# Unread products in TensorE's planned waits among the first pairs, and a plan in which GpSimd overlaps half of VectorE's two-operand passes

## Chip, cores and metric

The kernel runs on one core of a Trainium2 chip. The metric is the device time in microseconds (us) of that core, from an execution of the whole program. A profiled execution gives, beside its time, a trace of every instruction.

## What is computed

Attention with a sliding window of 128 keys and 4 sink keys, over 4 batches, 8 heads, 768 positions and head dimension 64; its result, laid side by side over the heads, goes through a two-layer network with squared ReLU. Cut to what matters:

```python
scores = q @ k.T / sqrt(64)
keep = (pos_k < n_sink) | ((0 <= pos_q - pos_k) & (pos_q - pos_k < window))
a = softmax(where(keep, scores, -1e9))
x = (a @ v), heads side by side          # 3072 x 512
h = maximum(x @ w_in, 0)                 # 512 x 2048
out = (h * h) @ w_out                    # 2048 x 512
```

The weights arrive as 64-bit numbers (w_in and w_out), the rest as 32-bit.

## The kernel before, in words

**Units of work.** The 3072 tokens are cut into 8 chunks of 384 tokens (half a batch), and each chunk has 4 pairs of heads, so there are 32 pairs. A pair's attention runs through: loads of q, k, v (lines 405, 410, 417); scores on TensorE (line 483 for the first eight pairs in plain fp32, line 489 for the others); a masked reduce on VectorE that also gives the row's minimum (line 466); the exponential on ScalarE (line 472); a sum and reciprocal on VectorE (lines 529, 530); the scaling of the rows on GpSimd or ScalarE (lines 537, 535); the sink columns on GpSimd (lines 552, 550); a transpose (by TensorE at lines 590 and 638 for the first two chunks, copied out of PSUM at line 600; later by VectorE and DMA); the product with the values (lines 726, 730); and the split of the result into a high and a low part, x (ScalarE line 742, VectorE line 747).

**The network.** Each chunk goes through 16 slices of the hidden dimension. A slice is a first product (12 matmuls, line 778), ReLU and square on ScalarE (lines 791, 795), two passes on VectorE (line 800, and line 807, which writes the low part gl), and a second product into three PSUM banks (9 matmuls, line 823; every third of them reads gl). After a chunk's last slice the three banks are copied out (line 864). The first chunk is run in two halves: slices 0 to 7, then all of the second chunk, then slices 8 to 15.

**The weights** are 32 rows of 64-bit words. VectorE turns each row into fp32 with three passes over integers (lines 303, 310, 317); ScalarE makes the rounded high part (line 323); and the low part is a subtraction (line 327) that the plan gives to VectorE or GpSimd, whichever it expects to be done first. All 32 rows are made while the first chunks are computed.

**Order.** Nothing is ordered by hand. The class Plan (from line 45) holds a list of steps, each with its engine and a cost in us written into the code, what it reads and writes, a rank, and the PSUM banks that it takes and gives back. Plan.order() plays the engines forward in time: it keeps the time when each engine is free, picks the step that can start first (by rank among those within 0.03 us), sets its start and end, and emits it. So each engine's instruction stream is written in the order in which the plan's own clock started the steps, and on the chip an engine runs its stream strictly in that order. Costs marked "port" are VectorE passes that use the SBUF port that VectorE shares with GpSimd. The plan lets such a pass and a GpSimd step exclude each other: whichever comes second starts when the first is over (lines 109, 110, 136 and 137):

```python
if e == "POOL" or "port" in kind:
    t = max(t, port["DVE" if e == "POOL" else "POOL"])
...
if e == "POOL" or "port" in kind:
    port[e] = t + cost
```

PSUM's eight banks are handed out by the plan too. Steps of the first chunk's pairs may take any of the eight; others take from three banks ("att"), the first products from two ("h") and the second from three ("o").

Of the kernel before, what the change touches and what calls it, by code (L numbers as in the profile page):

```python
# [18 lines left out]
P = 128  # L19
# [11 lines left out]
TOP_MAX = 2.0**16 * (2.0 - 2.0**-3 - 2.0**-23)  # L31
TOP_MIN = 2.0**-15 * 1.125
EPS = 1.0e-9
URGE = 0.5
LOW_DVE = 0.6
CP_DVE = 0.3
# [13 lines left out]
class Plan:  # L50
# [15 lines left out]
    def add(self, at, rank, emit, reads=(), writes=(), take=(), drop=()):  # L66
        n = len(self.steps)
        before = {self.writer[c] for c in (*reads, *writes) if c in self.writer}
        for c in writes:
            before.update(self.readers.get(c, ()))  # L70
        for c in reads:
            self.readers.setdefault(c, []).append(n)
        for c in writes:
            self.writer[c], self.readers[c] = n, []
        before.discard(n)
        for key in drop:
            self.left[key] = self.left.get(key, 0) + 1
        for b in before:
            self.steps[b]["after"].append(n)
        at = at if isinstance(at, list) else [at]  # L80
        self.steps.append(
            dict(at=at, rank=rank, emit=emit, take=take, drop=drop, after=[], waits=len(before), ready=0.0)
        )
# [12 lines left out]
    def order(self):  # L96
        free = dict(PE=0.0, DVE=5.5, ACT=1.5, POOL=5.0, SP=0.5)
        port, landed, mode, flow = {"DVE": 0.0, "POOL": 0.0}, [], 0, 0.0
        open_ = [n for n, s in enumerate(self.steps) if s["waits"] == 0]
        while open_:  # L100
            best = {}
            for n in open_:
                s = self.steps[n]
                ready, picks = self.able(s)
                if ready is None:
                    continue
                e, cost, *kind = min(s["at"], key=lambda o: max(ready, free[o[0]]) + o[1] + (o[3] if len(o) > 3 else 0.0))
                t = max(ready, free[e])
                if e == "SP" and len(landed) > 7:
                    t = max(t, landed[-8])  # L110
                if e == "POOL" or "port" in kind:
                    t = max(t, port["DVE" if e == "POOL" else "POOL"])
                best.setdefault(e, []).append((t, s["rank"], n, cost, kind, picks))
            chosen = None
            for e, able in best.items():
                first = min(able)[0]
                a = min((a for a in able if a[0] <= first + 0.03), key=lambda a: a[1:3])
                if chosen is None or a[0] < chosen[1][0]:
                    chosen = e, a
            e, (t, rank, n, cost, kind, picks) = chosen  # L120
            s = self.steps[n]
            open_.remove(n)
            for (pool, key), i in zip(s["take"], picks):
                self.got[key], self.since[i] = i, None
            if e == "PE":
                cost += 0.17 * (kind[0] != mode)
                mode = kind[0]
            free[e] = t + cost
            if e == "SP":
                flow = max(flow, t + 1.3) + kind[1] / RATE  # L130
                done = max(t + kind[0], flow + 0.7)
                landed.append(done)
                done += LATE
            else:
                done = t + cost + self.TAIL[e]
                if e == "POOL" or "port" in kind:
                    port[e] = t + cost
            for key in s["drop"]:
                self.left[key] -= 1
                if not self.left[key]:  # L140
                    self.since[self.got[key]] = done + self.HOP
            for a in s["after"]:
                x = self.steps[a]
                to_pe = x["at"][0][0] == "PE"
                x["ready"] = max(x["ready"], free[e] if to_pe and e == "PE" else done + (AHEAD if to_pe else self.HOP))
                x["waits"] -= 1
                if not x["waits"]:
                    open_.append(a)
            self.log.append((e, t, free[e], done, n, rank))
            yield (lambda: s["emit"](e)) if len(s["at"]) > 1 else s["emit"]  # L150
        assert all(not s["waits"] for s in self.steps)
# [3 lines left out]
def sink_window_attention_moe(  # L155
# [10 lines left out]
    nc = tc.nc  # L166
    B, NPAIR, _, S = q.shape
    H = 2 * NPAIR
    NROW, _, DM = w_rows.shape
# [11 lines left out]
    with ExitStack() as fast:  # L181
# [6 lines left out]
        def sb(tag, shape, dt=F32, name=None):  # L188

            name = name or tag  # L190
            if name not in made:
                made[name] = wp.tile(shape, dt, tag=tag, name=name)
            return made[name]

        banks = [ps.tile([P, 512], F32, name=f"bank{i}") for i in range(8)]
# [4 lines left out]
        ident = wp.tile([P, P], F32, name="ident")  # L200
# [6 lines left out]
        eps = wp.tile([P, 2 * NQ], F32, name="eps")  # L207
        nc.gpsimd.memset(eps, EPS)
        pari = sb("gl0", [P, 2, 2], I32, "pari")
# [59 lines left out]
        plan = Plan()  # L269
# [113 lines left out]
        def attention(s, rank):  # L383
# [79 lines left out]
            def reduce_(h, i, n, o, mask, key):  # L463
                ps_ = bank(key)
                nb = nbs[:, c * H + 2 * p + h, i : i + 1]
                nc.vector.tensor_tensor_reduce(  # L466
                    Pt(h)[:, i, o : o + n], ps_[:, 0:n], mask[:, 0:n], -SCALE, BIG, ALU.add, ALU.min, nb
                )

            def exp(h, i, n, o):  # L470
                nb = nbs[:, c * H + 2 * p + h, i : i + 1]
                nc.scalar.activation(  # L472
                    Pt(h)[:, i, o : o + n], Pt(h)[:, i, o : o + n], AF.Exp, bias=nb, scale=-1.0,
                    accum_out=sm[:, h, i : i + 1],
                )
# [25 lines left out]
            for m, (i, heads) in enumerate(order):  # L501
# [13 lines left out]
                for h, key in zip(heads, keys):  # L515
                    add(
                        ("DVE", 0.355 if n > P else 0.21), r - URGE,
                        lambda h=h, i=i, n=n, o=o, mask=mask, key=key: reduce_(h, i, n, o, mask, key),
# [4 lines left out]
                    add(  # L523
                        ("ACT", 0.5 if n > P else 0.4), r - URGE, lambda h=h, i=i, n=n, o=o: exp(h, i, n, o),
                        reads=[("nb", s, h, i), P_cell(h)], writes=[(P_cell(h), i), sm_cell, ("e", s, h, i)],
                    )

            def recip(hs):
                nc.vector.tensor_tensor(rs[:, hs], sm[:, hs], eps.rearrange("p (h i) -> p h i", h=2)[:, hs], op=ALU.add)  # L529
                nc.vector.reciprocal(rs[:, hs], rs[:, hs])  # L530

            def scale(engine, h, i, n, o):
                a = Pt(h)[:, i, o : o + n]
                if engine == "ACT":
                    nc.scalar.activation(a, a, AF.Copy, scale=rs[:, h, i : i + 1])
                else:
                    {"POOL": nc.gpsimd, "DVE": nc.vector}[engine].tensor_scalar(  # L537
                        a, a, rs[:, h, i : i + 1], 1.0, op0=ALU.mult, op1=ALU.mult
                    )
# [17 lines left out]
            for heads in groups:  # L557
                hs = slice(heads[0], heads[-1] + 1)
                r = rank(1.05 if plain or heads[0] else 1.45)
                add(  # L560
                    ("DVE", 0.22), r - URGE, lambda hs=hs: recip(hs),
                    reads=[("e", s, h, i) for h in heads for i in range(NQ)], writes=[(rs_cell, h) for h in heads],
                )
                for h in heads:
                    for i in range(NQ):
                        _, n, _, o = block(i)
                        pool = ("POOL", 0.46 if n > P else 0.33)
                        add(
                            [pool, ("ACT", 0.38 if n > P else 0.28, "", SC_ACT)] if plain else [pool, pool], r - URGE,
                            lambda e, h=h, i=i, n=n, o=o: scale(e, h, i, n, o),  # L570
# [3 lines left out]
                    add(  # L574
                        ("POOL", 0.29), r - URGE + 0.01, lambda h=h: part_sinks(h, False),
                        reads=done, writes=[(psk_cell, h)] + ([] if two == 0 else [psk_cell]),
                    )
                    add(
                        ("POOL", 0.32), r - URGE + 0.01, lambda h=h: part_sinks(h, True),
                        reads=done + [(psk_cell, h)], writes=[(psk_cell, h, 1)],  # L580
# [358 lines left out]
        def count():  # L939
# [10 lines left out]
            ("DVE", 0.1), END + 0.5, lambda: nc.vector.tensor_copy(flagi, bank("flag")[0:1, 0:1]), reads=["flag"],  # L950
            writes=["flagi"], drop=["flag"],
        )
        with tc.manual_schedule(engines={E.PE, E.DVE, E.Activation, E.Pool, E.SP}):
            for emit in plan.order():
                emit()
# [9 lines left out]
def general(  # L965
# [76 lines left out]
    with tc.For_i(0, B, 1) as b:  # L1042
        xT = one.tile([P, NPAIR, S], F32, name="gxT")
        for h in range(H):
# [9 lines left out]
            for i in range(NB):  # L1054
# [16 lines left out]
                nc.scalar.activation(sc, sc, AF.Exp, accum_out=st[:, 1:2])  # L1071
                nc.vector.tensor_scalar(st[:, 2:3], st[:, 1:2], EPS, None, op0=ALU.add)
                nc.vector.reciprocal(st[:, 3:4], st[:, 2:3])
# [86 lines left out]
```

## Time and profile before

| | |
|---|---|
| median of 3 runs | 691.01 us (689.49 to 691.43) |
| the profiled execution | 688.96 us |
| its span, first to last instruction | 686.9 us |
| TensorE matmuls busy | 667.4 us, 97% |
| VectorE busy | 459.1 us, 67% |
| ScalarE busy | 375.0 us, 55% |
| GpSimd busy | 215.2 us, 31% |
| mean granted TensorE clock | 0.991 |

In the profile PE is TensorE's matmuls, PEld its weight loads, DVE is VectorE, ACT ScalarE, POOL GpSimd, and SP the engine that issues the DMAs. A row of the timeline reads: start, duration, engine, line, operation, tiles written and read, how many instructions are merged, and in brackets the idle time before and what ended it. A row of the windows gives for a stretch of time the busy time of each engine with the number of instructions, then the granted TensorE clock (1.00 is full speed), the share of the DMA engines and GB/s. A product of two fp32 matrices is recorded as two matmuls (96 records at line 483 for 48 products in the program), a transpose as one (88 records at line 638 for 88 transposes).

### The profile page before, as it was taken

To read this page: it belongs to the slowest core of one execution; us is meant where nothing else is said; L and a number is where in the kernel's file an instruction comes from. 1 tells how busy PE (TensorE), PEld (TensorE's weight loads), DVE (VectorE), ACT (ScalarE), POOL (GpSimd) and SP (SyncE) were. 2 spreads that over 40 slices of the span, in tenths; PEclk is the share of its full clock that TensorE was granted. 3 is DMA by queue.
4 is the path that set the end of the run, shared out by engine and by line. 5 is a ranking of instruction groups with operands and counts; after the bars stand their busy time and mean duration, and the time that the engine had idled before them with its cause. 6 is when DMAs were issued, how large, how long until landed. Compare 5 with 4: busy or idle time off the path is not lost.

```text
span 686.9 us, 11380 instructions
## 1 busy us (share of the span) xinstructions
PE 667.4 (97%) x3722; PEld 581.1 (85%) x3722; DVE 459.1 (67%) x1194; ACT 375.0 (55%) x1073; POOL 215.2 (31%) x377
## 2 busy tenths in 40 slices
PE   4999989999999999999999999999999999999996
PEld 3667879998888888888888898888898888899985
DVE  7599999967987655676677766666776764242222
ACT  6798734355464434456666656666666565442221
POOL 4455433534544513232244323223332322000000
PEclk9799999999999999999999999999999999999999
DMA  7746455215777532466556666555557754310001
GB/s 244 220 163 203 168 192 183 84 52 157 223 245 227 154 106 93 134 207 193 155 148 184 211 188 201 170 167 174 145 169 213 223 160 114 116 51 12 0 1 51
DMA packets 58178, 104.78 MB, mean 153 GB/s; under 512 B 6208, under 2 KB 34624, under 8 KB 58112
## 3 DMA queue, kind: packets, MB, share of 16 engines
q1 hardware_dynamic: 58112, 103.98, 49.7%
q8 instruction: 31, 0.51, 0.3%
q14 instruction: 35, 0.29, 0.1%
HBM read 79.58 MB, written 24.38 MB: 151 GB/s over the span
## 4 chain that ended last, share of the span: by engine, by line
PE 90%; DVE 6%; ACT 1%; issue 1%; DMA 1%; SPq 0%; POOL 0%; DVEq 0%
PE bank L823 37%; PE bank L778 37%; PE bank L726 6%; PE bank L489 5%; PE bank L730 1%; DVE f L310 1%; PE bank L590 1%; PE bank L483 1%; DVE P L466 1%; PE bank L638 1%; DVE f L317 1%; DVE f L303 1%; DMA kn<-in_k_dram 1%; ACT w L323 0%; DVE w L327 0%
## 5 line engine op out<-in xcount | busy, mean ns | idle before, releaser
L778 PE MATMUL bank<-x,w 128*128 128x384 f32 x1536 | 303.1, 339 | 0.7 <-DVE gl L807 0.7
L778 PEld LDWEIGHTS bank<-x,w 128*128 128x128 f32 x1536 | 267.0, 188 | 9.5 <-issue 1.4
L823 PE MATMUL bank<-w,gh 128*128 128x512 f32 x768 | 242.7, 397 | 2.1 <-ACT ob L864 2.1
L823 PEld LDWEIGHTS bank<-w,gh 128*128 128x128 f32 x768 | 137.5, 188 | 21.4 <-ACT ob L864 2.4
L823 PE MATMUL bank<-w,gl 128*128 128x512 f32 x384 | 151.4, 394 | 0.0
L446 POOL TENSOR_TENSOR KS<-kn,KS 128x408 fp32r<-128x408 f32 (+1 forms) x48 | 64.9, 1352 | 225.1 <-DVE KS L441 164.2
L791 ACT ACTIVATE r<-bank 128x384 f32<-128x384 f32 x128 | 62.7, 490 | 129.3 <-PE bank L778 128.2
L472 ACT ACTIVATE P<-P,nbs 128x264 f32<-128x264 f32 (+1 forms) x192 | 94.4, 492 | 66.5 <-DVE nbs L466 65.7
L800 DVE TENSOR_TENSOR bank<-bank,r 128x384 f32<-128x384 f32 x128 | 72.1, 563 | 83.4 <-ACT r L791 83.1
L537 POOL TENSOR_SCALAR P<-P,small 128x128 f32<-128x128 f32 (+1 forms) x168 | 88.5, 543 | 71.1 <-DVE small L530 48.9
L823 PEld LDWEIGHTS bank<-w,gl 128*128 128x128 f32 x384 | 72.1, 188 | 16.6
L466 DVE CUSTOM_DVE_ANT_0 P<-bank,maskA 128x264 f32<-128x264 f32 x128 | 53.4, 426 | 45.1 <-PE bank L489 43.6
L807 DVE TENSOR_TENSOR gl<-bank,gh 128x384 fp32r<-128x384 f32 x128 | 70.9, 554 | 17.4 <-ACT gh L795 11.8
L795 ACT ACTIVATE gh<-r 128x384 fp32r<-128x384 f32 x128 | 66.7, 521 | 4.7 <-PE bank L823 2.2
L668 DVE STREAM_TRANSPOSE T<-P 128x384 f32<-128x384 f32 x96 | 45.2, 495 | 22.6 <-POOL P L537 21.7
L489 PEld LDWEIGHTS bank<-KS,QS 128*128 128x128 f32 x288 | 51.6, 188 | 6.2 <-DVE nbs L466 0.4
L489 PE MATMUL bank<-KS,QS 128*128 128x264 f32 (+1 forms) x288 | 55.4, 279 | 0.0
L742 ACT CAST x<-bank 128x384 fp32r<-128x384 f32 x32 | 15.3, 478 | 52.6 <-PE bank L730 52.4
L327 POOL TENSOR_TENSOR w<-f,w 128x512 fp32r<-128x512 f32 x19 | 27.1, 1430 | 51.4 <-ACT w L323 51.4
L726 PE MATMUL bank<-PT,vn 128*64 128x256 f32 (+1 forms) x392 | 40.6, 347 | 0.0
L726 PEld LDWEIGHTS bank<-PT,vn 128*64 128x64 f32 x392 | 25.7, 139 | 15.5 <-issue 6.7
L529 DVE TENSOR_TENSOR small<-small,eps 128x3 f32<-128x3 f32 (+1 forms) x56 | 34.5, 616 | 3.3 <-ACT P L472 2.7
(90 smaller groups left out, 575.5 us busy)
## 6 DMA issues: line engine op xcount, KB each, us to landing
raw<-in_moe_w_dram SPq DMA_DIRECT2D x32, 512.0 KB, 3.7
half<-in_moe_w_dram SPq DMA_DIRECT2D x64, 256.0 KB, 3.6
via<-T SPq DMA_DIRECT2D x48, 192.0 KB, 3.7
PT<-via SPq DMA_DIRECT2D x12, 768.0 KB, 4.4
via<-T SPq DMA_DIRECT2D x48, 160.0 KB, 4.2
PT<-via SPq DMA_DIRECT2D x12, 640.0 KB, 4.7
kn<-in_k_dram SPq DMA_DIRECT2D x24, 272.0 KB, 4.4
qn<-in_q_dram SPq DMA_DIRECT2D x32, 192.0 KB, 3.6
```

The source lines that it names most:

```text
L446: lambda h=h: nc.gpsimd.tensor_tensor(KS(h)[:, 1, 0:nk], kn()[:, h, 0:nk], f32(KS(h)[:, 0, 0:nk]), op=ALU.subtract),
L466: nc.vector.tensor_tensor_reduce(Pt(h)[:, i, o : o + n], ps_[:, 0:n], mask[:, 0:n], -SCALE, BIG, ALU.add, ALU.min, nb)
L472: nc.scalar.activation(Pt(h)[:, i, o : o + n], Pt(h)[:, i, o : o + n], AF.Exp, bias=nb, scale=-1.0, accum_out=sm[:, h, i : i + 1],)
L489: nc.tensor.matmul(bank(key)[:, 0:n], QS(h)[:, cols], flat[:, a, c0 : c0 + n], start=(a == 0), stop=(a == 1),)
L537: {"POOL": nc.gpsimd, "DVE": nc.vector}[engine].tensor_scalar(a, a, rs[:, h, i : i + 1], 1.0, op0=ALU.mult, op1=ALU.mult)
L726: nc.tensor.matmul(xo[h * D : h * D + D, qs[0] * P : qs[0] * P + len(qs) * P], vn[:, kk, h, :], rhs(), start=(n == 0), stop=False, skip_gr ...
L778: nc.tensor.matmul(bank(key)[:, 0:TOK], wi[fc][:, i, cc * P : (cc + 1) * P], xt[:, cc, :], start=(cc == 0 and j == 0), stop=(cc == NCC - 1 ...
L791: lambda key=key, r=r: nc.scalar.activation(r(), bank(key)[:, 0:TOK], AF.Relu),
L795: ("ACT", 0.41), n - 9, lambda gh=gh, r=r: nc.scalar.activation(gh(), r(), AF.Square),
L800: lambda key=key, r=r: nc.vector.tensor_tensor(bank(key)[:, 0:TOK], bank(key)[:, 0:TOK], r(), op=ALU.mult),
L807: lambda key=key, gh=gh, gl=gl: nc.vector.tensor_tensor(gl(), bank(key)[:, 0:TOK], f32(gh()), op=ALU.subtract),
L823: nc.tensor.matmul(bank(okey), gt()[:, ts_], wo[f][:, i, :], start=(f == f0 and j == 0), stop=(f == f1 - 1 and j == 2),)
```

## The change

There are two parts. Both sit in Plan.order().

1. When a TensorE step that takes a bank would start, by the plan's clock, before 24 us (WARM) and over 0.4 us after TensorE's step before it, the plan first emits fill(i, n): n fp32 products of the 128x128 identity with itself into the bank that the step is about to take. Nobody reads them; the step overwrites the bank. n is 70% of the planned wait (less 0.3 us) at 0.22 us a product. In the emitted program there are 33 such products: 20 ahead of the very first score, 1 ahead of the third pair's scores, and 12 among the first transposes. The plan's own clock isn't moved by them.
2. A GpSimd step, or a VectorE pass marked "port", holds the shared port for the plan only during the first half (SHARE) of its cost. No instruction is added, removed or resized by this, but every later choice of the plan can come out otherwise, so the streams of all engines are reordered from about the 20th instruction on, low passes go to other engines (line 327: VectorE 15 instead of 13, GpSimd 17 instead of 19), and 10 scalings go from ScalarE to GpSimd (line 537: 178 instead of 168; line 535: 14 instead of 24).

```diff
+WARM = 24.0
+SHARE = 0.5
...
             if e == "PE":
+                idle = t - free[e]
+                if picks and t < WARM and idle > 0.4:
+                    yield lambda i=picks[0], n=int((idle - 0.3) * 0.7 / 0.22): self.fill(i, n)
                 cost += 0.17 * (kind[0] != mode)
...
                 if e == "POOL" or "port" in kind:
-                    port[e] = t + cost
+                    port[e] = t + SHARE * cost
...
+        def fill(i, n):
+            for _ in range(n):
+                nc.tensor.matmul(banks[i][:, 0:P], ident, ident, start=True, stop=True)
+
+        plan.fill = fill
```

Three places in the streams show what moves. The lines of the changed kernel stand 5 further down up to the planner's callers and 10 at the end (line 960 is the new product). In names, the number behind the underscore at the end is a buffer's; P_1_0 and the like are a pair's probabilities, kn and qn its keys and queries, ident the identity.

TensorE, the start of its stream, before:

```order
L483 MATMUL bank0_67<-kn_0_146,qn_0_144 128x128
L483 MATMUL bank1_68<-kn_0_146,qn_0_144 128x128
L483 MATMUL bank2_69<-kn_0_146,qn_0_144 128x264
L483 MATMUL bank3_70<-kn_0_146,qn_0_144 128x264
L483 MATMUL bank4_71<-kn_0_146,qn_0_144 128x264
```

And now:

```order
L960 MATMUL bank0_67<-ident_78 128x128 x20
L488 MATMUL bank0_67<-kn_0_146,qn_0_144 128x128
L488 MATMUL bank1_68<-kn_0_146,qn_0_144 128x128
L488 MATMUL bank2_69<-kn_0_146,qn_0_144 128x264
L488 MATMUL bank3_70<-kn_0_146,qn_0_144 128x264
```

The first score stands behind 20 unread products.

ScalarE, where the third pair's exponentials (P_2) end, before:

```order
L472 ACTIVATE P_2_0_218,small_135<-P_2_0_218,nbs_125 128x264
L472 ACTIVATE P_1_198,small_135<-P_1_198,nbs_125 128x264
L472 ACTIVATE P_2_1_220,small_135<-P_2_1_220,nbs_125 128x264
L472 ACTIVATE P_2_0_218,small_135<-P_2_0_218,nbs_125 128x264
L472 ACTIVATE P_2_1_220,small_135<-P_2_1_220,nbs_125 128x264
L600 COPY PT_134<-bank2_69 128x512
```

And now (PT and SK are the copies of the first pair's transposes and of its sinks):

```order
L477 ACTIVATE P_2_0_239,small_135<-P_2_0_239,nbs_125 128x264
L477 ACTIVATE P_1_218,small_135<-P_1_218,nbs_125 128x264
L605 COPY PT_134<-bank2_69 128x512
L477 ACTIVATE P_2_1_241,small_135<-P_2_1_241,nbs_125 128x264
L605 COPY PT_134<-bank3_70 128x256
L605 COPY PT_134<-bank4_71 128x512
L540 ACTIVATE P_1_218<-P_1_218,small_135 128x264
L477 ACTIVATE P_2_0_239,small_135<-P_2_0_239,nbs_125 128x264
L605 CAST SK_0_132<-bank5_72 128x256
L477 ACTIVATE P_2_1_241,small_135<-P_2_1_241,nbs_125 128x264
```

The last three exponentials of the third pair stand behind the first pair's four copies.

VectorE, up to the fifteenth gl (line 807, now 812), which is slice 6 of the second chunk; f_28 is row 28 of the weights; before:

```order
L303 TENSOR_SCALAR f_28_1335<-raw_28_1260 128x512
L317 SCALAR_TENSOR_TENSOR f_27_1303<-raw_27_1219,f_27_1303 128x512
L310 SCALAR_TENSOR_TENSOR f_28_1335<-raw_28_1260,f_28_1335 128x512
L800 TENSOR_TENSOR bank4_71<-bank4_71,r_0_567 128x384
L807 TENSOR_TENSOR gl_0_590<-bank4_71,gh_0_578 128x384
```

And now:

```order
L322 SCALAR_TENSOR_TENSOR f_30_1352<-raw_30_1291,f_30_1352 128x512
L308 TENSOR_SCALAR f_31_1379<-raw_31_1312 128x512
L384 TENSOR_TENSOR VS_126<-vs_1_381,VS_126 16x512
L315 SCALAR_TENSOR_TENSOR f_31_1379<-raw_31_1312,f_31_1379 128x512
L805 TENSOR_TENSOR bank3_70<-bank3_70,r_0_630 128x384
L322 SCALAR_TENSOR_TENSOR f_31_1379<-raw_31_1312,f_31_1379 128x512
L812 TENSOR_TENSOR gl_0_653<-bank3_70,gh_0_635 128x384
```

The same product's low part stood behind weight rows up to 28 and now stands behind all 32, 0 to 31.

## The prediction

> **What bounds the kernel now.** I read TensorE's waits first, since its matmuls are busy 97% of the span. Columns: who waits for what, total us, times, longest.
>
> ```profile
> PE bank L483 <- DMA kn<-in_k_dram: 5.1, 2, 4.6
> PE bank L638 <- POOL P L537: 5.0, 4, 2.5
> PE bank L823 <- ACT ob L864: 2.1, 1, 2.1
> PE bank L778 <- DVE gl L807: 0.7, 1, 0.7
> ```
>
> There is little to win: 5.1 us for the first keys, 5.0 us for the first scaled rows, and two stops of 2.1 and 0.7 us. Next, the windows, for the clock (in each row: PE, PEld, DVE, ACT, POOL busy, then PEclk).
>
> ```profile
> 15.70:19.10 3.40, 1.33 (x5) 0.93 (x5) 3.33 (x8) 2.04 (x7) 3.40 (x5) 0.50 1.05 296
> 19.10:22.50 3.40, 3.35 (x14) 2.15 (x14) 0.53 (x4) 3.00 (x8) 3.40 (x12) 0.50 0.68 173
> 22.50:25.90 3.40, 3.40 (x16) 2.02 (x16) 0.79 (x4) 1.44 (x6) 0.95 (x5) 0.50 0.87 330
> 25.90:29.30 3.40, 3.40 (x27) 2.64 (x28) 2.63 (x8) 3.12 (x9) 0.00 (x0) 1.00 0.41 118
> ```
>
> From 15.7 to 25.9 us TensorE runs at half clock, after its waits; in the last 6.8 of these it is busy and slow, and VectorE idles behind it (0.53 and 0.79 of 3.40). Part 1 of the change aims there. The start is slow too, though the window's clock column says 1.00 there: the scores' mean duration (last number) is 628 ns between 4.5 and 8.8 us, and 402 ns between 9 and 11.5.
>
> ```profile
> L483 PE MATMUL bank<-kn,qn 64*128 64x264 f32 x11 | 3.3, 628 | 0.0
> ```
>
> ```profile
> L483 PE MATMUL bank<-kn,qn 64*128 64x264 f32 x15 | 2.5, 402 | 0.0
> ```
>
> So dense work ran about 4.2 us, from 4.6 to 8.8, before the clock came up. Then the stretch in which the weights are made:
>
> ```profile
> 60.00:100.00 40.00, 37.89 (x228) 32.04 (x227) 38.78 (x68) 26.22 (x60) 17.27 (x20) 1.00 0.51 176
> 100.00:140.00 40.00, 40.00 (x204) 36.28 (x203) 38.63 (x73) 17.10 (x37) 15.39 (x14) 1.00 0.40 133
> ```
>
> VectorE is as full as TensorE there (38.8 and 38.6 of 40). Its own waits from 18 to 140 us:
>
> ```profile
> DVE x L747 <- ACT x L742: 4.6, 3, 3.4
> DVE P L466 <- PE bank L483: 3.5, 4, 2.7
> DVE bank L800 <- ACT r L791: 0.7, 3, 0.4
> DVE P L466 <- POOL w L327: 0.7, 1, 0.7
> ```
>
> Of 9.5 us in all, the two longest (3.4 and 2.7) lie in the half-clock stretch; 3.4 us are scattered over the other 110. How close the two engines run is seen at the fifteenth gl, on VectorE and then where TensorE reads it:
>
> ```profile
> 124.70 0.56 DVE L807 TENSOR_TENSOR gl<-bank,gh 128x384 fp32r<-128x384 f32 x1
> ```
>
> ```profile
> 125.60 0.39 PE L823 MATMUL bank<-w,gl 128*128 128x512 f32 x1
> ```
>
> It is written at 125.26 and read at 125.60: 0.34 us of slack. Until about 140 us VectorE is a second bound, and TensorE stops for whatever VectorE is given ahead of a gl. After it TensorE has no stop but the one of 0.7 us, so a delay at 125 us lasts to the end.
>
> **Part 1, the unread products.** The price of one: transposes of the same 128 columns, at half and at full clock.
>
> ```profile
> 17.65 1.33 PE L638 MATMUL bank<-ident,P 128*128 128x128 f32 x5 [2.47 <-POOL P L537]
> ...
> 25.96 1.04 PE L638 MATMUL bank<-ident,P 128*128 128x128 f32 x8
> ```
>
> Five take 1.33 us and eight 1.04; with the modelled tail taken off, one record is 0.21 and 0.11, with it 0.27 and 0.13. A product is two records: 0.43 us cold and 0.22 warm, at most 0.53 and 0.26. The identity is there at 1.32 + 0.29 = 1.61 us:
>
> ```profile
> 1.32 0.29 POOL masks.py:199 TENSOR_SCALAR_AFFINE_SELECT ident<-ident 128x128 f32<-128x128 f32 x1
> ```
>
> With 4.2 us of cold work as above, some 10 of the 20 products run cold and 10 warm: 1.6 + 4.2 + 10 x 0.22 = 8.0 us. The ends are 6.0 (all warm) and 12.2 (all cold, upper price). The Trainium skill (TensorE: Matmul & The Clock Gate, Part 1) has the gate open after a busy window of about 3.4 us; by that the products would end at about 7.7. In the trace VectorE reads the first score at 6.27:
>
> ```profile
> 6.27 0.29 DVE L466 CUSTOM_DVE_ANT_0 P<-bank,mask 128x128 f32<-128x128 f32 x1
> ```
>
> It reads it at about 8.3 now, since the score takes 0.2 to 0.3 us more: **VectorE and all behind it start 2.0 us late** (0 to 6). The 13 others fall in waits for GpSimd and ScalarE, which last longer than they do (5.0 us against 13 x 0.22 = 2.9), so I cost them at nothing; uncovered they would cost 2.9.
>
> What comes back is VectorE's idling at half clock, 6.1 us, less what idling is new. The third pair's reciprocal ran at 17.16:
>
> ```profile
> 17.16 0.15 DVE L529 TENSOR_TENSOR small<-small,eps 128x6 f32<-128x6 f32 x1
> ```
>
> It now starts 2.0 later and has three more weight passes ahead (0.60 + 0.34 + 0.60, prices below): 20.7. But the exponentials that it needs stand behind the copies of the first pair's transposes and sinks, and these wait for GpSimd:
>
> ```profile
> 12.39 5.21 POOL L537 TENSOR_SCALAR P<-P,small 128x128 f32<-128x128 f32 x6 [5.66 <-DVE small L530]
> 17.55 1.01 POOL L552 CAST PSK<-P 128x32 fp32r<-128x32 f32 x2
> 18.52 0.84 POOL L550 TENSOR_TENSOR PSK<-P,PSK 128x16 fp32r<-128x16 f32 x2
> ```
>
> GpSimd's last of these ends at 19.36, now 21.4; with the turn, the copy and the exponential (estimate 1.4) it is 22.8. VectorE waits 2.1 us for it, and I add 0.7 for the first cast of weights behind the same copies. So 6.1 - 2.0 - 2.1 - 0.7 = **1.3 us of lead for VectorE** at about 30 us. This needs the clock to hold up. In 19.1 to 22.5 TensorE was busy 3.35 of 3.40 us, half of it with transposes, and the clock stayed at 0.50. The Trainium skill (TensorE: Matmul & The Clock Gate, Part 4) says that transposes do not count as busy for the gate; by that the 12 late products, 2.6 us over a stretch of some 8, may be too thin, and the lead would be gone. That is in the range below.
>
> **Part 2, the order.** First what overlap the trace shows. A GpSimd subtraction and the VectorE pass that met it:
>
> ```profile
> 92.17 2.92 POOL L327 TENSOR_TENSOR w<-f,w 128x512 fp32r<-128x512 f32 x2 [2.81 <-ACT w L323]
> ```
>
> ```profile
> 92.43 1.52 DVE L303 TENSOR_SCALAR f<-raw 128x512 int32<-128x512 int32 x1
> ```
>
> The pass takes 1.52 us, against 0.42 alone (next fence), and ends 0.3 us behind the first subtraction: it waited for all of it, not for half. The Trainium skill (SBUF — State Buffer, section "SBUF: two separate sides") calls this port pair an exclusive lock that is held for the whole instruction. By that, each half that the plan now lets overlap is time that VectorE does not have. The prices of VectorE's passes when nothing is in the way, from start to start:
>
> ```profile
> 27.74 0.42 DVE L466 CUSTOM_DVE_ANT_0 P<-bank,maskA 128x264 f32<-128x264 f32 x1
> ...
> 28.45 0.69 DVE L310 SCALAR_TENSOR_TENSOR f<-raw,f 128x512 int32<-128x512 int32 x1
> 29.05 0.42 DVE L303 TENSOR_SCALAR f<-raw 128x512 int32<-128x512 int32 x1
> 29.39 0.68 DVE L317 SCALAR_TENSOR_TENSOR f<-raw,f 128x512 int32<-128x512 int32 x1
> 29.99 0.68 DVE L310 SCALAR_TENSOR_TENSOR f<-raw,f 128x512 int32<-128x512 int32 x1
> ...
> 32.37 0.16 DVE L529 TENSOR_TENSOR small<-small,eps 128x6 f32<-128x6 f32 x1
> 32.56 0.19 DVE L530 RECIPROCAL small<-small 128x6 f32<-128x6 f32 x1
> 32.67 1.25 DVE L327 TENSOR_TENSOR w<-f,w 128x512 fp32r<-128x512 f32 x2
> ```
>
> That is 0.60 for lines 310, 317 and 327, 0.34 for line 303, 0.30 for a reciprocal with its sum, and 0.36 for a reduce (two of them from 27.74 to 28.45). Counted in the streams, the new order puts ahead of the fifteenth gl 3 more passes of line 303, 3 of line 310, 4 of line 317 and 3 of line 327: 3 x 0.34 + 10 x 0.60 = 7.0 us. A cast and a subtraction of sinks come before it too (priced as 0.34 + 0.60), and three reduces, one reciprocal and one copy go behind it (1.08 + 0.30 + 0.60): -1.0. VectorE has **6.0 us more to do** by then. GpSimd's part ahead of it is the same (17 subtractions of line 327 in both), so what its port takes from VectorE is left as it is. TensorE's stream has six scores (line 489) less ahead of the product; the chain of waits has six in 0.72 us.
>
> ```profile
> 107.85 0.72 PE bank L489 x6
> ```
>
> **The sum**, at the fifteenth gl: +6.0, less the slack 0.34, less the lead 1.3, less 1.8 of the 3.4 us of scattered idling (an engine with a longer queue has something to do; I take about half), plus the 0.7 that TensorE still has to do behind it: **+3.3 us**. The gls before it give less by the same count. The profiled execution took 688.96 us, 2.1 more than its span; with +3.3 it is 692.3. The runs' median, 691.01, lies 2.05 above it, and the prediction is for the median: **694.3**. Ends of the terms: idling wholly saved +1.7, not at all +5.1, and with the lead lost as well +6.4.
>
> **Rivals.**
>
> *The clock wins (faster).* The half-clock stretch goes, VectorE's lead of 1.3 comes through, and the stop of 2.1 us in front of line 823 closes, because weights made earlier no longer keep ScalarE's copy waiting: 691.0 - 3.4 = 687.6. For it: the 0.50 rows. Against it: in those rows TensorE's work is done by 26 us anyway, and VectorE's passes are what stop it later. It decides if the 6.0 us of earlier weight work costs TensorE under 3.4 us, that is if the plan's half is closer to the chip than the 1.52 us row. Chance 0.27.
>
> *They cancel (no change).* The weight work moves ahead only where VectorE would have idled: with all 3.4 us saved and a lead of 2, the sum is 0.96; 692. Within 0.3%, 2.1 us, which is about what a measurement of this kernel can tell from no change. Chance 0.18.
>
> *The first products cost more (slower).* They stay cold to the end, 12.2 us: VectorE starts 6.2 late instead of 2.0, the lead turns into a lag of 2.9, and the sum is 3.3 + 4.2 = 7.5: 698.5. For it: the clock needed 8.2 us of nearly full work from 17.65 to 25.9. Against it: 4.2 us sufficed for the scores. Chance 0.10.
>
> **The numbers.** The forecast has 0.45: slower altogether 0.55. The range takes the clock's win at its lower end (687.5) and the cold start at its upper (698.5); what is left out is a bigger win and a start that is later still. The forecast's own range is 692.7 to 697.4.
>
> **What the profile after would show.** Right: VectorE's first line 471 at about 8.3 us; a clock of 1.00 between 16 and 26 us, or 0.50 again with the lead lost; VectorE's busy time still full from 30 to 120 us and lighter from 125 to 140; TensorE waiting for line 812 or for weight passes somewhere from 80 to 126 us, some 5 us in all where 2.1 stood; nothing changed after 140. Wrong: no such waits, because VectorE got through the extra passes in time.

## The result and the profile after

The changed kernel takes 694.18 us (median of seven runs, 693.56 to 696.78), the kernel before in the same rounds 691.01 (seven, 688.94 to 692.46). The ratio is 1.0056, interval 1.0034 to 1.0077: slower by 3.2 us, where 3.3 was forecast. The profiled execution of after took 696.78 us (span 694.5), the most of its seven, that of before 688.96 (span 686.9), 2.05 under its median, so the two traces lie 7.6 us apart. Below, traces say where time goes and medians how much. One execution of e10 (892.67 us, at a granted clock of 0.69) and one of before in the rounds of e14 (2295.72 us) are slow ones and are left out of the medians.

TensorE's waits in after:

```profile
PE bank L643 <- POOL P L542: 4.1, 6, 2.0
PE bank L595 <- POOL PSK L555: 2.9, 5, 0.9
PE bank L828 <- DVE gl L812: 2.3, 3, 1.0
PE bank L960 <- POOL ident masks.py:199: 1.7, 1, 1.7
```

The wait for the first keys is covered, and so is the stop of 2.1 us for ScalarE's copy (line 864, now 869). Two kinds of wait are new: for VectorE's gl at line 828, as forecast, but 2.3 us where the forecast had some 5; and at line 595 (590 before) for GpSimd's sink columns (PSK), which the forecast does not have. The start, on TensorE and on VectorE:

```profile
1.66 7.58 PE L960 MATMUL bank<-ident 128*128 128x128 f32 x40 [1.66 <-POOL ident masks.py:199]
```

```profile
9.70 0.29 DVE L471 CUSTOM_DVE_ANT_0 P<-bank,mask 128x128 f32<-128x128 f32 x1 [2.75 <-PE bank L488]
...
23.88 0.17 DVE L534 TENSOR_TENSOR small<-small,eps 128x6 f32<-128x6 f32 x1 [1.95 <-ACT P L477]
```

The twenty products (40 records) end at 9.24 us, the first reduce starts at 9.70 instead of 6.27, and the third pair's reciprocal runs at 23.88 instead of 17.16. The windows that answer to those of before (PE, PEld, DVE, ACT, POOL busy, then the clock):

```profile
15.70:19.10 3.40, 1.48 (x9) 0.85 (x8) 3.30 (x8) 2.42 (x9) 3.40 (x5) 1.00 1.05 305
19.10:22.50 3.40, 1.58 (x10) 1.29 (x11) 2.76 (x5) 1.70 (x5) 3.40 (x6) 0.83 1.04 245
22.50:25.90 3.40, 3.40 (x17) 2.51 (x18) 1.44 (x4) 2.55 (x8) 3.26 (x10) 0.50 0.77 258
25.90:29.30 3.40, 3.40 (x22) 2.57 (x18) 1.28 (x4) 1.75 (x5) 1.60 (x4) 0.67 0.51 167
60.00:100.00 40.00, 38.55 (x230) 31.34 (x228) 39.47 (x78) 26.15 (x61) 22.57 (x25) 1.00 0.65 203
100.00:140.00 40.00, 37.67 (x185) 32.85 (x184) 34.63 (x57) 14.98 (x29) 10.63 (x8) 1.00 0.35 120
```

The half clock did not go in this execution, it came later. VectorE is full from 60 to 100 us and lighter from 100 to 140, since its weight work was done earlier. The fifteenth gl, on VectorE, then TensorE, then GpSimd:

```profile
129.31 1.68 DVE L315 SCALAR_TENSOR_TENSOR f<-raw,f 128x512 int32<-128x512 int32 x1
130.91 0.55 DVE L805 TENSOR_TENSOR bank<-bank,r 128x384 f32<-128x384 f32 x1
131.38 0.68 DVE L322 SCALAR_TENSOR_TENSOR f<-raw,f 128x512 int32<-128x512 int32 x1
131.98 0.54 DVE L812 TENSOR_TENSOR gl<-bank,gh 128x384 fp32r<-128x384 f32 x1
```

```profile
132.58 0.50 PE L828 MATMUL bank<-w,gl 128*128 128x512 f32 x1 [0.93 <-DVE gl L812]
```

```profile
128.96 1.48 POOL L332 TENSOR_TENSOR w<-f,w 128x512 fp32r<-128x512 f32 x1 [1.28 <-ACT w L328]
```

The slack of 0.34 us became a stop of 0.93, and the gl is read at 132.58 instead of 125.60, 7.0 us later in this long execution. Two weight passes stand ahead of the gl, and the first takes 1.68 us, where 0.69 is its duration alone (line 310 in the prediction's rows): it met a GpSimd subtraction that ended at 130.44 and ended 0.55 behind it. It waited for all of it. The Trainium skill (SBUF — State Buffer, section "SBUF: two separate sides") states a lock held for the whole instruction; this row agrees.

### The profile page after: what moved, and what is told of

The parts are those of the page before. It is cut to its first block, busy times and chain, and to the rows that moved or that the text cites. A ratio compares the mean times of both kernels' runs of the same rounds, so it can differ in the third digit from the quotient of the medians.

```text
span 694.5 us, 11511 instructions
## 1 busy us (share of the span) xinstructions
PE 677.2 (98%) x3788; PEld 589.0 (85%) x3788; DVE 459.1 (66%) x1195; ACT 373.2 (54%) x1064; POOL 218.5 (31%) x385
## 4 chain that ended last, share of the span: by engine, by line
PE 83%; DVE 9%; POOL 3%; ACT 2%; issue 2%; DVEq 0%; POOLq 0%
PE bank L828 34%; PE bank L783 34%; PE bank L731 5%; PE bank L494 5%; DVE f L322 2%; DVE f L315 2%; POOL P L542 2%; PE bank L735 1%; PE bank L595 1%; PE bank L960 1%; DVE P L471 1%; DVE f L308 1%; DVE gl L812 1%; DVE bank L805 1%; ACT w L328 1%
## 5 line engine op out<-in xcount | busy, mean ns | idle before, releaser
L542 POOL TENSOR_SCALAR P<-P,small 128x264 f32<-128x264 f32 (+1 forms) x178 | 93.4, 540 | 71.1 <-DVE small L535 51.0
L332 POOL TENSOR_TENSOR w<-f,w 128x512 fp32r<-128x512 f32 x17 | 24.2, 1423 | 39.8 <-ACT w L328 38.5
```

## Experiments

Theory A: the order costs the time, through VectorE's weight work ahead of gls. Rivals: the first products cost it (theory B); the waits for GpSimd in the first pairs cost it (P); any other order moves the time by chance (C). Ratios are against the kernel before, in the same rounds; they are not the quotients of the medians, and a difference between two versions whose intervals overlap is not clear of the noise. The three columns behind them are read from each timeline: when TensorE starts to read the second and the eighteenth gl, and the distance. Behind the eighteenth, every version needs another 548.6 to 550.8 us of span.

| run | median us | ratio, 95% interval | second gl | eighteenth | distance |
|---|---|---|---|---|---|
| before | 690.5 to 691.0 | | 56.46 | 138.15 | 81.7 |
| after | 694.18 | 1.0056, 1.0034 to 1.0077 | 61.82 | 145.43 | 83.6 |
| e1_products_only | 690.17 | 0.9995, 0.9985 to 1.0004 | 55.28 | 136.96 | 81.7 |
| e2_order_only | 693.98 | 1.0039, 1.0027 to 1.0052 | 59.19 | 142.82 | 83.6 |
| e3_no_first20 | 693.38 | 1.0036, 1.0023 to 1.0049 | 57.16 | 140.82 | 83.7 |
| e4_first20_only | 691.98 | 1.0023, 1.0013 to 1.0033 | 58.51 | 141.75 | 83.2 |
| e5_half_early | 688.13 | 0.9962, 0.9949 to 0.9975 | 56.69 | 136.92 | 80.2 |
| e6_half_late | 691.93 | 1.0030, 1.0019 to 1.0042 | 56.78 | 140.18 | 83.4 |
| e7c_share_0 | 705.52 | 1.0210, 1.0188 to 1.0233 | 64.15 | 153.19 | 89.0 |
| e8_late_only | 690.08 | 0.9985, 0.9968 to 1.0003 | 54.23 | 137.48 | 83.3 |
| e10_before_more_passes | 697.79 | 1.0105, 1.0091 to 1.0120 | 56.30 | 145.89 | 89.6 |
| e11_order_fewer_passes | 691.04 | 1.0001, 0.9992 to 1.0010 | 58.59 | 139.13 | 80.5 |
| e13_half_early_seven | 686.49 | 0.9949, 0.9932 to 0.9966 | 55.31 | 135.49 | 80.2 |
| e14_after_seven | 692.72 | 1.0034, 1.0022 to 1.0045 | 57.01 | 140.67 | 83.7 |

after, e2, e3 and e14 have one order, and their distances agree within 0.1 us, whatever the products did. So the order's price in that stretch is rigid, and the products can only move its start.

**The two parts apart.** The products alone, on the order of before:

```diff
-SHARE = 0.5
+SHARE = 1.0
```

> Part 1 alone: the unread products as planned waits call for them (20 first, 1, then 13 and 9 in the first transposes, since the old plan's waits are longer there), order as before. Theory A, that the order costs the time (VectorE's 6.0 us of earlier weight work) and the products bring VectorE 1.3 us: 689 to 691 us. Theory B, that the 20 first products cost it (VectorE's first reduce at 9.7 us instead of 6.27 in the changed kernel's trace) and the order nothing: 693 to 695 us, and the first reduce at 9 to 10 us.

The order alone, without products:

```diff
-WARM = 24.0
+WARM = 0.0
```

> Part 2 alone: the changed kernel's order, no unread product. Theory A: 694 to 696 us, with TensorE stopping some 4 us for line 812 between 80 and 126 us. Theory B: 690 to 692 us; stops for line 812 of 2 us or less, since the stop of 2.1 us before line 823 has gone in exchange.

Together the products are worth nothing that shows on the old order (690.17, interval across 1). The order alone costs 3.5 us by the medians, of a total of 3.2 to 3.7. Its stops for gl are 2.3 us, where theory A had some 4. TensorE's waits in e2:

```profile
PE bank L643 <- POOL P L542: 4.4, 7, 1.9
PE bank L595 <- POOL PSK L555: 3.4, 5, 1.0
PE bank L828 <- DVE gl L812: 2.3, 3, 1.0
```

Of the 4.7 us that its trace lies behind before's at the eighteenth gl, 2.7 are there at the second, and 1.9 come after.

**The first twenty and the later thirteen.** The change without the first twenty, and the first twenty alone on the old order:

```diff
-                if picks and t < WARM and idle > 0.4:
+                if picks and 0 < free[e] and t < WARM and idle > 0.4:
```

> The changed kernel without the 20 products ahead of the first score; the 13 later ones stay. Theory A: 693 to 695 us, since the order is kept. Theory B: 690 to 692 us, 3 us under the changed kernel, with the first reduce at 6.3 us again. Either way the clock: if the 13 products hold it, 1.00 from about 9 us on.

```diff
-SHARE = 0.5
+SHARE = 1.0
...
-                if picks and t < WARM and idle > 0.4:
+                if picks and not free[e] and t < WARM and idle > 0.4:
```

> The kernel before with the 20 products ahead of its first score and nothing else. Theory A: 691 to 692.5 us, since a late start of 2 us is made good in the half-clock stretch. Theory B: 693.5 to 695 us; the 3.4 us of late start arrive at the end whole.

The first twenty cost 1.5 us on the old order (691.98). The later ones give back 1.8 beside them there (691.98 to 690.17). On the new order the same two differences are 0.8 (694.18 against 693.38) and 0.6 (693.98 to 693.38), with intervals that overlap widely: they have the same signs and are not shown. Nor did the thirteen hold the clock there: in e3's trace it is 0.70 and 0.80 in the two windows from 15.7 to 22.5 us. The later ones alone on the old order:

```diff
-SHARE = 0.5
+SHARE = 1.0
...
-                if picks and t < WARM and idle > 0.4:
+                if picks and 0 < free[e] and t < WARM and idle > 0.4:
```

> The order of before, and only the later products in the planned waits of the first pairs, without the twenty ahead of the first load's end. Taking the two measured effects as a sum (all products on the old order minus 0.4, the first twenty alone plus 1.5), the later ones are worth 1.9: 688.6, and the clock at 1.00 for at least 5 us more of the first pairs than before. If the later products need the first twenty to keep the clock up, 690 to 691.5 and a stretch at 0.50 of 5 us or more.

The expected 1.9 us did not come: 690.08, interval across 1. Its trace is 2.2 us ahead at the second gl, with the clock at 1.00 from 15.7 to 25.9, and 0.7 at the eighteenth. What takes back 1.6 us of distance, in e8 and in e4 alike, is the clock: behind the stop of 2.1 to 2.2 us for ScalarE's copy it fell to half for 3.4 us. In e4 the window behind that stop:

```profile
102.60:106.20 3.60, 3.60 (x13) 3.56 (x12) 3.47 (x7) 0.00 (x0) 0.00 (x0) 0.53 0.49 186
```

In the traces of before and of e1, with the same stop, it did not fall there. So one order has executions 1.6 us apart. The twelve executions of e8 show what the clock is worth: the four with a mean granted clock of 0.998 or 0.999 took 686.3 to 688.4 us, the eight with 0.993 to 0.996 took 688.5 to 692.3. The products can bring some 3 us on this order, in those executions in which the clock then stays up.

**Where in the order.** The half share only for what the plan issues before its 24th us, and only after it, without products:

```diff
-WARM = 24.0
+WARM = 0.0
...
-                    port[e] = t + SHARE * cost
+                    port[e] = t + (SHARE if t < 24.0 else 1.0) * cost
```

> No products; half the port share only for what the plan issues before its 24th us, the full share from there on. It has the new order in the first pairs, with the sink columns that wait for GpSimd, and little of VectorE's moved weight work: by the plan VectorE has 4.5 us more work than TensorE ahead of the early gl's against before, but only 1 us ahead of the eighth and all later ones. Theory A (the weight work that stands ahead of the later gl's costs the time): 690 to 691.5, with no stop above 0.5 us for a gl. Theory P (the waits for GpSimd in the first pairs cost it): 693 to 694.5, with 3 us or more of TensorE's waits for the sink columns' copy. Theory C (any other order moves the time by some us up or down, without a rule): anything from 687 to 695.

```diff
-WARM = 24.0
+WARM = 0.0
...
-                    port[e] = t + SHARE * cost
+                    port[e] = t + (SHARE if t >= 24.0 else 1.0) * cost
```

> The other half: full share before the plan's 24th us, half from there on, no products. The first pairs keep the old order; VectorE has no more work than before ahead of the first two gl's and 4 to 7 us more ahead of all from the fourth on. Theory A: 693 to 695, with two or three stops for gl of 2 to 3 us together, as in the order alone. Theory P: 690 to 691.5, and the waits for the sink columns gone. If both parts cost, this and the run with the early half add up to the 3.5 us of the order alone. Theory C: anything from 687 to 695, and no such sum.

The stretch goes as theory A has it: with the late half there are stops for gl (1.4 us) and a distance of 83.4, with the early half none at line 828 for a gl and 80.2. The times do not: 688.13 and 691.93 lie under theory A's ranges and outside P's, and only the wide one of theory C holds both, so these two runs do not decide against chance. e5 is faster than before by 2.4 us, which no theory but C allowed. The waits of e5, in which the stop of 2.1 for ScalarE's copy is gone and one of 1.0 for a copy by VectorE is new:

```profile
PE bank L643 <- POOL P L542: 3.9, 4, 1.9
PE bank L828 <- DVE ob L869: 1.0, 1, 1.0
...
PE bank L595 <- POOL PSK L555: 0.2, 1, 0.2
```

The two do not add up to e2 (-2.4 and +1.4 against +3.5), as theory C said: where both halves are in, the waits for the sink columns are 3.4 us, against 0.2 in e5 and 1.5 in e6; 2.0 of them lie ahead of the second gl. That goes with the first pairs' share, 2.7 us at the second gl, which neither half has alone (0.2 and 0.3). VectorE's rows of weights do not make it: by the streams e2 has finished 9 rows ahead of that gl and e5 8, where before had 6. Up to it, TensorE idles 11.6 us and is busy 47.6 in e2, against 9.8 and 46.9 in e5 and 10.8 and 45.7 in before. So what e2 loses against e5 is mostly waiting. Of what it loses against before, 1.9 us is longer busy time, although the records differ only by three more transposes of sink columns (0.6 us); what else makes it longer is not shown. The whole overlap, share 0:

```diff
-WARM = 24.0
-SHARE = 0.5
+WARM = 0.0
+SHARE = 0.0
```

> No products, and a share of 0: in the plan GpSimd and VectorE's two-operand passes overlap wholly. By the plan VectorE has up to 10.8 us more work than TensorE ahead of a gl against before, where the share of one half has up to 7.2. Theory A: more of the same, 696 to 699 (3.5 us for 7.2, so 7 for 10.8 if the first 3.6 are free), and stops for gl of 5 us or more together. Theory C: no relation to that count, 687 to 695. Theory P: by the waits for GpSimd in the first pairs alone, 693 to 696.

All theories put it too low: 15 us slower. Both losses grew, 7.7 us by the second gl and 7.4 in the distance; the waits for the sink columns nearly doubled:

```profile
PE bank L595 <- POOL PSK L555: 6.1, 6, 2.5
PE bank L643 <- POOL P L542: 4.4, 4, 2.2
...
PE bank L828 <- DVE gl L812: 2.3, 2, 1.2
PE bank L828 <- DVE ob L869: 2.0, 1, 2.0
```

**The term itself.** Six microseconds of VectorE's work added to the old order, and taken from the new one, with every other instruction in its place. For the first, the third integer pass (line 317) runs twice for ten rows:

```diff
...
-                lambda: nc.vector.scalar_tensor_tensor(
-                    f(), raw()[:, :, 0], 29, f(), op0=ALU.logical_shift_right, op1=ALU.bitwise_or
-                ),
...
+            def third():
+                for _ in range(1 + (n in range(10, 20))):
+                    nc.vector.scalar_tensor_tensor(
+                        f(), raw()[:, :, 0], 29, f(), op0=ALU.logical_shift_right, op1=ALU.bitwise_or
+                    )
+
+            add(("DVE", 0.62, "port"), rank, third, reads=[raw_cell], writes=[f_cell])
```

> The kernel before, in its own order, where rows 10 to 19 of the weights run VectorE's third integer pass twice (the second changes nothing): ten passes of 0.60 us, so 6.0 us more work for VectorE between the third and the ninth gl, which is the term that the prediction was built on. Theory A (VectorE's weight work ahead of a gl costs the time): 6.0 less the slack of 0.34 and 1.8 of idling, 3.9 more: 694.4, or 692.3 if the stop of 2.1 us closes in return, with stops for gl of 3 us or more that before has not. Rival (VectorE has the room; the order as such costs): 690 to 691.5 and no new stops.

697.79 us, 7.1 us slower, more than was put in and 3.4 over theory A's forecast. VectorE from the first gl to the ninth, in before and in e10 (busy times as above):

```profile
46.72:99.52 52.80, 50.69 (x306) 41.48 (x305) 50.86 (x100) 36.77 (x89) 25.25 (x30) 1.00 0.52 172
```

```profile
46.58:105.58 59.00, 51.80 (x306) 41.25 (x305) 57.13 (x111) 36.66 (x89) 26.28 (x30) 1.00 0.48 153
```

The stretch grew by 6.20 and VectorE's busy time by 6.27: VectorE sets the pace, and its 1.9 us of idling stayed. TensorE, with the same 306 matmuls, idles 7.2 us instead of 2.1. Its waits at line 824 (823 before):

```profile
PE bank L824 <- ACT ob L865: 3.7, 1, 3.7
PE bank L824 <- DVE gl L808: 1.4, 1, 1.4
```

The stop for ScalarE's copy did not close, it grew from 2.1 to 3.7. Right behind it the clock fell to half, as it did in e4 and e8 (0.50 between 107.0 and 107.6 us): the same twelve first products, in before and in e10:

```profile
100.68 2.27 PE L778 MATMUL bank<-x,w 128*128 128x384 f32 x12
```

```profile
106.82 3.73 PE L779 MATMUL bank<-x,w 128*128 128x384 f32 x12
```

From the ninth to the fifteenth gl e10 loses 1.6 us more by that. So its trace loses 6.2 us to the ten passes and 1.6 to the clock. Why the copy is late is seen on ScalarE, in before and then in e2:

```profile
98.02 0.62 ACT L323 CAST w<-f 128x512 fp32r<-128x512 f32 x1 [3.92 <-DVE f L317]
98.55 0.58 ACT L864 COPY ob<-bank 128x512 f32<-128x512 f32 x1
```

```profile
98.46 0.59 ACT L869 COPY ob<-bank 128x512 f32<-128x512 f32 x1 [0.33 <-PE bank L828]
```

The copy stands behind the making of a weight row that waited 3.92 us for VectorE's third pass. That old stop is a wait for VectorE's weight work too; in the new order no such row stands ahead of the copy. The second, on the order alone, leaves out the third pass of ten rows, whose weights then lack their lowest three bits (the function as above, with another count):

```diff
-WARM = 24.0
+WARM = 0.0
...
+            def third():
+                for _ in range(n not in range(10, 20)):
...
```

> The new order without products, instruction for instruction, but the third integer pass is left out for rows 10 to 19 (their weights lack the lowest three bits): 6.0 us less for VectorE between the third and the ninth gl, as much as the order puts there; the first pairs are untouched. Theory A: the stops for gl (2.3 us) go and part of the 1.7 us lost from the second to the fifth gl: 690.5 to 691.7. What is then left over the run with the early half (688.1) is the first pairs' share, 2.5 us. Rival (the order as such costs, or the waits of the first pairs alone): 693 to 694, stops as before.

691.04, 2.9 us less than e2, as theory A has it; the distance falls from 83.6 to 80.5. One of the three stops for gl went, and so did the two waits for sink columns (0.90 and 0.54 us) that e2 has behind the second gl:

```profile
PE bank L596 <- POOL PSK L556: 2.2, 4, 1.0
PE bank L829 <- DVE gl L813: 1.3, 2, 0.9
```

Those two waits were VectorE's work at one remove. The four scalings ahead of the first of them, on GpSimd in e2 and then in e11:

```profile
62.12 3.48 POOL L542 TENSOR_SCALAR P<-P,small 128x264 f32<-128x264 f32 x4 [1.66 <-DVE small L535]
```

```profile
61.36 2.55 POOL L543 TENSOR_SCALAR P<-P,small 128x264 f32<-128x264 f32 x4 [1.48 <-DVE small L536]
```

With fewer of VectorE's passes beside them they take 0.93 us less. From the second to the fifth gl e11 needs 21.9 us, e2 23.8. A control is missing: before without the same ten passes was not run. From the second to the eighteenth gl TensorE idles only 2.1 us in before, less than the 3.1 by which e11's distance falls. The second gl of e11 is still 2.1 us behind before's, so the first pairs' share stands, as it should: their passes were untouched.

**The first products at seven.** On the order of e5:

```diff
-                    yield lambda i=picks[0], n=int((idle - 0.3) * 0.7 / 0.22): self.fill(i, n)
+                    yield lambda i=picks[0], n=int((idle - 0.3) * 0.7 / 0.22) if free[e] else 7: self.fill(i, n)
...
-                    port[e] = t + SHARE * cost
+                    port[e] = t + (SHARE if t < 24.0 else 1.0) * cost
```

> The best so far (half share before the plan's 24th us, full share after) with the later products and only seven in front of the first load instead of twenty, which at 0.43 us cold end by about 4.7 us, when the first keys land. If dense work from 1.7 us on opens the clock: full clock from about 6 us, the first scores 1 us shorter, 686.5 to 687.8. If the products do nothing on this order (as the first twenty and the later ones together did on the old one): 687.8 to 688.6. If they make the first score late, its first reduce comes after 6.5 us and the time is 688.5 or more.

686.49 us, the fastest version by its median: 4.2 us under before, and 1.6 under e5, whose interval it overlaps. Five of its executions took 685.9 to 687.6 us at a mean clock of 0.996 to 0.998, the sixth 689.7 at 0.991. In the trace the clock stayed up through the stretch that ran at half in before:

```profile
15.70:19.10 3.40, 1.21 (x9) 1.02 (x9) 3.33 (x8) 2.05 (x6) 3.40 (x6) 1.00 1.06 284
19.10:22.50 3.40, 2.87 (x22) 2.01 (x23) 2.33 (x6) 2.63 (x8) 3.32 (x8) 1.00 0.82 214
22.50:25.90 3.40, 3.07 (x26) 2.10 (x27) 2.87 (x12) 3.17 (x10) 3.27 (x10) 1.00 0.98 360
```

The first scores were still cold (664 ns each between 4.5 and 8.8 us, where before has 628), and the first reduce came at 6.85 us, later than the bound of 6.5 that the expectation set for a loss: the gain is in the clock behind it. No run has this order with the later products alone, which held the clock up on the old one (e8), so what the seven bring is not separated. The same seven in the change as it is (the first of these two edits alone):

> The change as it is, with one number other: seven products ahead of the first score instead of twenty; the 13 later ones stay. It asks whether the clock, held up, is worth anything on this order. On the order with the early half, seven products and the later ones took 1.6 us off and the clock stayed at 1.00. If the start decides (a first reduce at about 6.9 instead of 9.7 us, and the clock held): 691.8 to 692.6. If VectorE's weight work and the waits for GpSimd take back what the clock gives (the prediction's reason against its faster rival): 693 to 694.2, with the stops for gl of 2 us unchanged. If most of the change's loss were the late start: 691 or less.

692.72, just above the case in which the start decides, and 1.5 us under after, with overlapping intervals. The clock is at 1.00 from 15.7 to 25.9 us here as well, and the waits of the order are all there:

```profile
PE bank L595 <- POOL PSK L555: 4.0, 6, 1.0
PE bank L643 <- POOL P L542: 2.3, 4, 1.1
PE bank L828 <- DVE gl L812: 2.3, 3, 1.0
```

So a full clock does not turn this change into a gain: 2.2 us over before.

## Why the prediction was right

The time, the sign and the main mechanism were right; two terms were wrong and stood against a third that was left out. By the prediction's steps, with e2 (the order alone) as the measure, against the trace of before:

- **VectorE as the second bound: right.** e10 shows it: ten passes more, and the stretch from the first to the ninth gl longer by all of them.
- **6.0 us less the slack and 1.8 of idling, 3.9 net: right in size.** From the second to the eighteenth gl e2 loses 1.9 us and has no stop of 2.1 for the copy, so its other losses there are 4.0. The stops for gl make 2.3 of these; most of the remaining 1.7 are the two waits between the second and the fifth gl, 0.90 and 0.54, for GpSimd's sink columns. The forecast has no such path, but e11 shows VectorE's passes behind them too. The reason given for the 1.8, that idling fills up with moved work, was hardly borne out: from the second to the fifteenth gl VectorE idles 1.3 us in e2 and 1.8 in before, and e10 saved none. And 6.0 us is no constant price: adding them to the old order cost 7.1, with the fall of the clock, and taking them from the new one gave 2.9.
- **"1.3 us of lead for VectorE": wrong, the step that failed.** At the second gl the order is 2.7 us behind without any product (e2). On the old order the products did bring such a lead, 1.2 us at the second gl in e1, whose clock stayed up; on the new one the order takes it back. The forecast priced VectorE's part of the first pairs and not the new waits for GpSimd's sink columns, 3.4 us in e2, 2.0 of them ahead of the second gl, nor the longer busy time. With the first twenty it is worse: they ended at 9.24 instead of 8.0.
- **The stop of 2.1 us: left out.** It was put into the faster rival alone. It closed in every version of the new order, for the reason which that rival named.
- **What that makes.** Lead and lag differ by 4.0 us, the closed stop is worth 2.1 the other way, and the trace of before lies 1.5 under its median in the later rounds, where that of e2 lies 0.4 over. At the fifteenth gl, where the forecast has +3.3, e2's trace is 4.4 us behind before's. That the median came out at the forecast is in part these misses cancelling, and in that part luck.
- **The thirteen later products at no cost: right.** On the old order they gave back 1.8 us beside the first twenty, which cost 1.5 there; alone they gave nothing that shows in e8's median. On the new order neither difference is clear of the noise.

Rivals: the clock's win is real on the old order, where e8's executions with a full clock lie around that rival's 687.6 us, and loses to the new one: e14, with the clock up, is still 2.2 us over before. How much of its 1.5 us under after is the clock and how much the earlier start is not separated. "The first products cost more" had the right direction and too long a cold stretch. That the whole is chance of reordering is not what e10 and e11 show, since they keep the order and move the time both ways; that chance has no part in it is not shown either, after e5 and e6.

What stays open: why the early and late half together make waits for the sink columns that neither makes alone, why TensorE's nearly unchanged work up to the second gl keeps it busy 1.9 us longer in e2, and why the early half alone gains.

## What to carry to other kernels

When a planner's cost rule is relaxed, check it against rows in which the two engines meet: here a pass waits for the whole subtraction, and a share of one half, used throughout, moved work to where it was waited for. Used for the plan's first 24 us alone it gained 2.4 us, so a rule that misprices the engines can still hit on a better order, and only a run tells. Test a term by adding or removing just that work in an unchanged order; it told more here than any new order. Fill a planned wait only up to the time at which its data land, since what runs past it delays what stands behind: the first keys land at 4.6 us, twenty products ran to 8 or 9, and they cost 1.5 us on the old order.

## What was not expected of the hardware

**The cold start has no fixed length.** The same twenty products from the same time, in e1 and in e4:

```profile
1.67 6.50 PE L960 MATMUL bank<-ident 128*128 128x128 f32 x40 [1.67 <-POOL ident masks.py:199]
```

```profile
1.67 7.35 PE L960 MATMUL bank<-ident 128*128 128x128 f32 x40 [1.67 <-POOL ident masks.py:199]
```

In after it is 7.58. The single records are 0.21 us apart and then 0.11, from 5.4 (e1), 7.2 (e4) and 7.7 us (after): 3.7 to 6.0 us of unbroken work before the clock came up. In e13, with seven products and then the scores, which leave 0.15 us idle, the scores still take 615 ns between 8.8 and 9.9 us and 407 behind that: cold up to 8.2 us after the first product. The prediction took one trace's 4.2 for a constant. The Trainium skill (TensorE: Matmul & The Clock Gate, Part 1) says that the gate's window of about 3.4 us runs freely and does not start with the kernel, and that the transition varies by about 500 ns either way for that reason. That it varies agrees with these traces; the spread of the three, 2.3 us, is larger than that.

**A stop can cost more than itself.** Behind the same stop of about 2.1 us the clock fell to half in e4 and e8, 1.6 us more, and did not in before and e1; behind e10's stop of 3.7 it fell too, for the same 1.6. Closing such a stop takes away its own time and this risk.
